# The opening of a fused attention and feed-forward kernel: v of the first head pair on the SP queue, float32 opening matmuls, another order of the first hidden matmuls

## The chip, the cores and the metric

The kernel runs on one core of a Trainium2 chip. The core has TensorE (PE in the profile, with its weight loads listed apart as PEld), VectorE (DVE), ScalarE (ACT), GpSimd (POOL) and SyncE (SP), and 16 DMA engines. The metric is the device time of one execution in microseconds; lower is better. Six runs of the kernel before gave 287.94 to 288.43 us with a median of 288.18 us.

## What is computed

Inputs are float32: q, k, v of shape (8 batches, 8 heads, 576 tokens, 64), g_norm (64), w_in (512, 2048) and w_out (2048, 512). The output has 8 x 576 = 4608 rows of 512.

```python
kv  = einsum('bhsd,bhse->bhde', k, v)          # 64 x 64 per head, no softmax
o   = einsum('bhsd,bhde->bhse', q, kv)
o   = o / sqrt(mean(o*o, -1) + 1e-6) * g_norm  # per token and head
x   = o.transpose(0, 2, 1, 3).reshape(4608, 512)
h   = x @ w_in
out = (h * sigmoid(1.702 * h)) @ w_out
```

## The kernel before

Everything is cast to float16 on the way in and accumulated in float32 in PSUM. Heads go in pairs (`c` = 0 to 3), so that a pair fills 128 partitions. Each batch's first 512 tokens make one tile of the feed-forward part; the last 64 tokens of all eight batches together make a ninth. The 512 model columns are four slices of 128 (`ko` = 0 to 3, which are also the head pairs: slice `ko` of `x` is what the attention of pair `ko` leaves), and the 2048 hidden columns are 16 slices (`fo`). `Hidden.mm(ko, fo)` (L432) is one matmul of 128x128 weights `w_in_sb[:, ko, fo]` with 512 columns of `xT`; four of them over `ko` make one slice of `h`, which `gate` (L443) turns into `gT` on ACT. `project` (L468) multiplies `gT` with `w_out`.

The order of the work on each engine is the order of the program text (`manual_schedule`): every engine runs its own instructions strictly in that order, with semaphores where one needs another's result. The main loop over nine tiles `t` runs `dense(t)` on TensorE and puts the attention steps of batch `t + 1` between its matmuls. Batch 0 has no such cover: it is the opening, written out by hand (L548 to L614), and it is what this change is about.

The opening works like this. For each head pair c of batch 0:

- `a0.q(c)` (L386): 12 transposes of `qraw` on TensorE, copied to `qT` by DVE.
- `a0.kv(c)` (L368): 12 small matmuls of `kraw` and `vbuf`, whose sum DVE spreads into the block-diagonal `kvb` (a multiplication with `ones2`).
- `a0.out(c)` (L253): one matmul of `kvb` with `qT`, squared by ACT into `sq`.
- `a0.sums(c)` (L328), `a0.rs(c)` (L341), `a0.apply(c)` (L347): a matmul of `sq` with `ones2`, then Ln and Exp on ACT, then the product on DVE that writes slice c of `xT`.

Between these stand `busy(n)` calls (L556): n matmuls of 128x512 over the zeroed `kvb[1]`, into a PSUM tile that nobody reads. They keep TensorE running. Then `d0` computes the first six slices of `h` for tile 0 (L598 to L614), and the main loop takes over with slice 6.

Loads. Transfers that cast float32 to float16 are issued on POOL's queue (`early_load` L90, `load_w_in` L153, `load_w_out` L189, `load_half` L110); POOL computes the descriptors of each, about 0.63 us per load in the profile. The program keeps eight semaphores for this queue, in turn, so that a transfer waits until the eighth one ahead of it has landed. For pair 0 the kernel uses float32 transfers on the SP queue for k and q instead (L144 to L148), which are then cast on DVE (`kraw`, L551) and ACT (`qraw`, L550). The order on POOL is: v of pair 0, q of pair 1, the identity matrix (`affine_select`, L162) and three memsets of `ones2` (L171 to L173), k and v of pair 1, then q, k, v of pairs 2 and 3, then w_in in five pieces: slices fo 0-3 with ko 0-1, fo 0-3 with ko 2-3, fo 4-5, fo 6-9, fo 10-15 (L177 to L181). After these come w_out and the data of batch 1.

Of the kernel before, what the change touches and what calls it, by code (L numbers as in the profile page):

```python
# [8 lines left out]
F32 = mybir.dt.float32  # L9
# [3 lines left out]
P = 128  # L13
# [3 lines left out]
def kernel(  # L17
# [10 lines left out]
    nc = tc.nc  # L28
# [6 lines left out]
    KO = DM // P  # L35
    EPS = 1e-6
    SM = 512
# [6 lines left out]
    PE_ = 96  # L44
    NJ = S // PE_
    GROUP = 6
# [5 lines left out]
    const = ctx.enter_context(tc.tile_pool(name="const", bufs=1))  # L52
# [7 lines left out]
    ps_o = ctx.enter_context(tc.tile_pool(name="ps_o", bufs=2, space=bass.MemoryType.PSUM))  # L60
# [13 lines left out]
    vbuf = const.tile([P, NPAIR, 2 * NJ * D], F16)  # L74
# [5 lines left out]
    w_in_sb = const.tile([P, KO, DFF], F16)  # L80
# [9 lines left out]
    def early_load(n, b, c0, c1):  # L90
        nc.gpsimd.dma_start(  # L91
            out=raw[n][0:PE_, c0:c1, :].rearrange("p c (l x) -> p (c l) x", l=2),
            in_=early_src(n, b, c0, c1),
        )
# [45 lines left out]


    first = {}
    early_load("v", 0, 0, 1)
    for n in "kq":  # L144
        first[n] = stage.tile([P, H, J * D], F32, name=f"{n}f", tag=f"{n}f")
        first[n] = first[n].rearrange("p h x -> p (h x)")[0:PE_, 0 : 2 * NJ * D]
        dst, src = first[n].rearrange("p (h x) -> p h x", h=2), early_src(n, 0, 0, 1)
        nc.sync.dma_start(out=dst, in_=src)  # L148
    g_row = const.tile([1, D], F32)
    nc.scalar.dma_start(out=g_row, in_=g_norm.unsqueeze(0))  # L150
    nc.vector.memset(ident, 0.0)
    nc.vector.memset(kvb[1], 0.0)
    def load_w_in(f0, f1, k0=0, k1=KO):  # L153
        nc.gpsimd.dma_start(  # L154
            out=w_in_sb[:, k0:k1, f0 * P : f1 * P],
            in_=moe_w_in[k0 * P : k1 * P, f0 * P : f1 * P].rearrange(
                "(ko ki) f -> ki ko f", ki=P
            ),
        )

    early_load("q", 0, 1, 2)
    nc.gpsimd.affine_select(  # L162
        out=ident,
        in_=ident,
# [6 lines left out]
    nc.gpsimd.memset(ones2, 0.0)  # L171
    nc.gpsimd.memset(ones2[0:D, 0:D], 1.0)
    nc.gpsimd.memset(ones2[D:P, D:P], 1.0)  # L173
    for c in range(1, NPAIR):
        for n in "qkv"[c == 1 :]:
            early_load(n, 0, c, c + 1)
    load_w_in(0, 4, 0, 2)  # L177
    load_w_in(0, 4, 2, KO)
# [267 lines left out]
    def dense(t, units1, units2, group, deep, hid=None):  # L446
# [21 lines left out]
        def project(mo, fo):  # L468
# [10 lines left out]
            if fo == FO - 1:  # L479
# [69 lines left out]

    nc.scalar.copy(qraw[0:PE_, 0, :], first["q"])  # L550
    nc.vector.tensor_copy(kraw[0:PE_, 0, :], first["k"])  # L551


    idle_ps = ps_h.tile([P, SM], F32, name="idle", tag="hT")

    def busy(n):  # L556
        for _ in range(n):
            nc.tensor.matmul(
                idle_ps,
                kvb[1][:, 0, :],  # L560
                kvb[1].rearrange("p c r -> p (c r)"),
                start=True,
                stop=True,
            )

    busy(12)
    a0.q(0)
    busy(2)
    a0.kv(0)
# [10 lines left out]
    a0.out(1)  # L580
    a0.q(2)
    a0.rs(0)
    busy(1)
    a0.kv(2)
    a0.sums(1)
    a0.apply(0)
    busy(1)
    a0.out(2)
    a0.rs(1)
    a0.q(3)  # L590
# [3 lines left out]
    a0.out(3)  # L594
    a0.rs(2)
    a0.apply(2)
    busy(3)
    d0 = Hidden(0)  # L598
    for fo in range(4):
        d0.mm(0, fo, *((ps_h, "hT") if fo < 3 else (ps_a, "att")))  # L600
        if fo == 2:
            a0.ss(3)
            a0.apply(3)
    for ko in (1, 2):
        for fo in range(4):
            d0.mm(ko, fo)
    for ko in range(KO - 1):
        d0.mm(ko, 4, ps_o, "o")
    for fo in range(GROUP - 1):
        d0.mm(KO - 1, fo)  # L610
    for ko in range(KO):
        d0.mm(ko, GROUP - 1, ps_o, "o")
    for fo in range(GROUP):
        d0.gate(fo)  # L614
    load_w_out(0, 4)
# [12 lines left out]
    nc.gpsimd.dma_start(out=g_all, in_=g_norm.unsqueeze(0).to_broadcast([P, D]))  # L628

    osbs = {}  # L630
    HALVED = (2, 3, 4, 5, 6, 7)
    live = {0: a0}

    def start(b):
# [2 lines left out]
    for t in range(NT):  # L637
# [12 lines left out]
        if t == 0:  # L650
# [8 lines left out]
            for c in range(NPAIR):  # L659
# [4 lines left out]
                o = (32, 35, 50, 53)[c]  # L664
# [5 lines left out]
        elif b < B:  # L670
# [5 lines left out]
            f0 = 5 if t == 1 else 2  # L676
# [48 lines left out]
```

## Time and profile before

| | |
|---|---|
| median of six runs | 288.18 us (287.94 to 288.43) |
| the profiled execution | 288.18 us |
| its span, first to last instruction | 286.4 us |
| granted TensorE clock, mean | 1.000 |
| TensorE matmul busy | 278.7 us (97%) |
| ScalarE busy | 156.1 us (54%) |
| VectorE busy | 118.3 us (41%) |
| GpSimd busy | 57.6 us (20%) |
| DMA moved | 38.61 MB, mean 135 GB/s |

All times in the views are microseconds from the start of the span. A timeline row gives the start, the length, the engine, the line of the kernel, the operation, what it writes and reads, how many instructions were merged, and in brackets how long the engine had been idle and what ended the wait. A row of the DMA queues gives packets, megabytes written and the time that the packets took as a share of 16 engines in that stretch; it can be over 100% since packets overlap in an engine. A row of the DMA issues ends with the time from issue to landing. An f16 load of 144 KB reads 288 KB of float32.

Two things help in reading the rows. First, a matmul's listed length (379 ns for 128x512) holds its latency; the spacing of such matmuls in a run is what they cost, and it is 0.216 us where TensorE is at full speed. Second, "busy" in the last 255 us is nearly the whole of TensorE's time, so only the first 30 us leave TensorE waiting.

### The profile page before, as it was taken

How to read it: one execution, taken by the hardware profiler on the slowest of the kernel's cores; microseconds unless marked ns; L12 is line 12 of the kernel's file. 1: busy time of each engine (PE TensorE's matmuls, PEld its weight loads, DVE VectorE, ACT ScalarE, POOL GpSimd, SP SyncE). 2: the span in 40 equal slices, each digit the busy share in tenths (PEclk: the TensorE clock that was granted, in tenths of full speed). 3: DMA queues.
4: the chain of work that ended last, by engine and by line, in shares of the span. 5: the costliest groups of instructions: out<-in, count | busy, mean ns of one | idle time of the engine just before them, and what ended most of it. 6: DMA issues, size and time to landing. Idle time of an engine off the chain costs nothing.

```text
span 286.4 us, 4353 instructions
## 1 busy us (share of the span) xinstructions
PE 278.7 (97%) x1717; PEld 134.8 (47%) x1717; DVE 118.3 (41%) x229; ACT 156.1 (54%) x273; POOL 57.6 (20%) x83
## 2 busy tenths in 40 slices
PE   7799999999999999999999999999999999999995
PEld 2344554455445544554455445544455444444443
DVE  1460466617671567147713853276427500110001
ACT  2588538866565745584467526763666365016400
POOL 8842362111211121113011401131001100000000
PEclk9999999999999999999999999999999999999999
DMA  8999999996589448972798269925401310020022
GB/s 155 169 205 206 205 227 247 235 271 117 124 171 248 80 108 154 229 145 55 209 198 173 38 206 159 227 45 170 95 2 35 112 76 0 36 88 25 0 73 73
DMA packets 54214, 38.61 MB, mean 135 GB/s; under 512 B 31235, under 2 KB 50947, under 8 KB 54195
## 3 DMA queue, kind: packets, MB, share of 16 engines
q0 software_dynamic: 15168, 15.73, 34.0%
q1 hardware_dynamic: 38624, 22.09, 30.3%
q10 hardware_dynamic: 402, 0.52, 0.6%
q8 instruction: 13, 0.21, 0.3%
q14 instruction: 7, 0.05, 0.1%
HBM read 36.73 MB, written 9.44 MB: 161 GB/s over the span
## 4 chain that ended last, share of the span: by engine, by line
PE 92%; DMA 3%; POOL 3%; issue 1%; DVE 0%; POOLq 0%
PE hT L435 43%; PE o L472 42%; DMA w_in_sb<-in_moe_w_in_dram 3%; PE kvp L224 3%; PE outR L288 2%; PE oh L504 1%; POOL vbuf L91 1%; POOL qraw L91 1%; PE ss L336 1%; POOL kraw L91 1%; PE q L413 0%; PE outT L267 0%; PE outT L256 0%; POOL w_in_sb L154 0%; POOL ident L162 0%
## 5 line engine op out<-in xcount | busy, mean ns | idle before, releaser
L472 PE MATMUL o<-w_out_sb,gT 128*128 128x512 f16 x560 | 130.7, 379 | 0.0
L444 ACT ACTIVATE gT<-hT 128x512 f16<-128x512 f32 x144 | 84.5, 599 | 77.1 <-PE hT L435 77.0
L435 PE MATMUL hT<-xT,w_in_sb 128*128 128x512 f16 x512 | 116.3, 379 | 0.3 <-DMA w_in_sb<-in_moe_w_in_dram 0.2
L435 PEld LDWEIGHTS <-w_in_sb 128*128 128x128 f16 x576 | 54.4, 98 | 63.0 <-DMA w_in_sb<-in_moe_w_in_dram 1.4
L472 PEld LDWEIGHTS <-gT 128*128 128x128 f16 x560 | 52.9, 98 | 56.3
L482 DVE COPY osb<-o 128x512 f32<-128x512 f32 x20 | 13.8, 691 | 62.4 <-PE o L472 62.4
L320 POOL TENSOR_TENSOR x<-xr,g_all 128x512 f16<-128x512 f32 x12 | 15.2, 1270 | 70.2 <-DVE xr L313 52.1
L215 DVE COPY kpad<-kraw 64x576 f16<-64x576 f16 x56 | 25.0, 446 | 1.7 <-DMA kraw<-in_k_dram 0.5
L299 DVE TENSOR_REDUCE sum<-sq 128x8 f32<-128x512 f16 x24 | 15.8, 678 | 19.9 <-ACT sq L296 19.9
L237 DVE CAST kvb<-kvp 64x128 f16<-64x128 f32 x28 | 8.1, 288 | 36.8 <-PE kvp L224 36.6
L313 DVE TENSOR_TENSOR xr<-outR,sum 128x512 f32<-128x512 f32 x24 | 15.5, 686 | 11.1 <-ACT sum L310 11.1
L112 POOL DMA_DIRECT2D kraw<-in_k_dram x16 | 9.9, 624 | 49.1 <-DVE kpad L215 42.8
L112 POOL DMA_DIRECT2D vbuf<-in_v_dram x16 | 9.7, 608 | 35.3 <-PE kvp L224 29.6
L320 DVE TENSOR_TENSOR x<-xr,g_all 128x512 f16<-128x512 f32 x12 | 15.2, 1266 | 0.7
L296 ACT ACTIVATE sq<-outR 128x512 f16<-128x512 f32 x24 | 13.6, 590 | 2.0 <-PE outR L288 1.6
L224 PEld LDWEIGHTS <-kpad 128*128 128x128 f16 x252 | 11.1, 98 | 6.5 <-DVE kpad L215 0.2
L435 PE MATMUL hT<-x_rem,w_in_sb 128*128 128x512 f16 x64 | 14.0, 379 | 0.0
L276 ACT ACTIVATE sq<-outT 128x512 f16<-128x512 f32 (+1 forms) x16 | 7.7, 480 | 10.3 <-PE outT L256 8.9
L338 ACT ACTIVATE ln<-ss,eps_t 128x512 f32<-128x512 f32 (+1 forms) x16 | 9.4, 584 | 5.3 <-PE ss L336 5.3
L482 ACT COPY osb<-o 128x512 f32<-128x512 f32 x15 | 8.7, 581 | 6.3 <-PE o L472 6.3
L224 PE MATMUL kvp<-vbuf,kpad 128*128 128x64 f16 x252 | 11.9, 193 | 0.0
L309 ACT ACTIVATE sum<-sum,eps_t 128x16 f32<-128x16 f32 x12 | 3.7, 308 | 15.0 <-DVE sum L299 14.9
(61 smaller groups left out, 140.3 us busy)
## 6 DMA issues: line engine op xcount, KB each, us to landing
out_dram<-osb SPq DMA_DIRECT2D x12, 512.0 KB, 2.8
qf<-in_q_dram SPq DMA_DIRECT2D x5, 1024.0 KB, 8.6
kraw<-in_k_dram POOLq DMA_DIRECT2D x12, 288.0 KB, 6.0
vbuf<-in_v_dram POOLq DMA_DIRECT2D x12, 288.0 KB, 5.6
w_out_sb<-in_moe_w_out_dram POOLq DMA_DIRECT2D x3, 512.0 KB, 14.8
vbuf<-in_v_dram POOLq DMA_DIRECT2D x8, 144.0 KB, 6.6
out_dram<-osb SPq DMA_DIRECT2D x6, 192.0 KB, 4.0
qf<-in_q_dram POOLq DMA_DIRECT2D x1, 1024.0 KB, 11.6
```

What stands on the lines that cost most here:

```text
L112: nc.gpsimd.dma_start(out=raw[n][l * PH : (l + 1) * PH, c0:c1, 0 : NH * D], in_=srcs[n][b].rearrange("(c l) (p j) d -> l p c (j d)", l=2, ...
L215: nc.vector.tensor_copy(out=kpad[r, c, :, l * D : (l + 1) * D], in_=kraw[r, c, 0 : NH * D].rearrange("p (j d) -> p j d", j=NH),)
L224: nc.tensor.matmul(self.kvp[:, c, :], kpad[:, c, j, :], vbuf[:, c, j * D : (j + 1) * D], start=(j == 0), stop=(j == NH - 1),)
L296: nc.scalar.activation(sq, t, AFT.Square)
L299: nc.vector.tensor_reduce(out=self.sum2[:, j % 2, :], in_=sq.rearrange("p (h d) -> p h d", h=H), op=ALU.add, axis=mybir.AxisListType.X,)
L313: nc.vector.tensor_mul(xr[:, i], self.o[j + i].rearrange("p (h d) -> p h d", h=H), s2[:, i, :].unsqueeze(2).to_broadcast([P, H, D]),)
L320: (nc.vector if i else nc.gpsimd).tensor_mul(self.x16[:, j + i, :].rearrange("p (h d) -> p h d", h=H), xr[:, i], g_all.unsqueeze(1).to_bro ...
L338: nc.scalar.activation(ln[:, 0:n], t[:, 0:n], AFT.Ln, bias=eps_t, scale=1.0 / D)
L435: nc.tensor.matmul(self.h[fo], w_in_sb[:, ko, fo * P : (fo + 1) * P], self.x[:, ko], start=(ko == 0), stop=(ko == KO - 1),)
L444: nc.scalar.activation(self.gT[:, fo, :], self.h[fo], AFT.Gelu_apprx_sigmoid)
L472: nc.tensor.matmul(os[mo], gT[:, fo, mo * P : (mo + 1) * P], w_out_sb[:, fo, :], start=(fo == 0), stop=(fo == FO - 1),)
L482: copy(osb[:, mo, :], os[mo])
```

## The change

Pair 0's v goes onto the SP queue as a third float32 transfer behind k and q, and DVE casts it to `vbuf` (behind the cast of k and ahead of the copy of `qT` of pair 0). POOL's queue loses that load, and q of pair 1 is no longer ahead of the identity and the memsets but behind them. The twelve opening float16 matmuls become three float32 ones over a new zeroed tile. Of the later filler matmuls, the two `busy(1)` go, and `busy(3)` becomes `busy(1)`. The first 24 hidden matmuls are the same, in another order: ko 0, 1, 2, 3 of slices 0 to 3, then slices 4 and 5 whole; before, three matmuls of slice 4 stood between ko 2 and ko 3. Tile 7 is stored with one transfer at its end and not with two.

```diff
-    early_load("v", 0, 0, 1)
-    for n in "kq":
+    for n in "kqv":
         first[n] = stage.tile([P, H, J * D], F32, name=f"{n}f", tag=f"{n}f")
...
     nc.vector.memset(ident, 0.0)
+    zeros = const.tile([P, SM], F32)
+    nc.vector.memset(zeros, 0.0)
     nc.vector.memset(kvb[1], 0.0)
...
-    early_load("q", 0, 1, 2)
     nc.gpsimd.affine_select(
...
     nc.gpsimd.memset(ones2[D:P, D:P], 1.0)
...
     for c in range(1, NPAIR):
-        for n in "qkv"[c == 1 :]:
+        for n in "qkv":
             early_load(n, 0, c, c + 1)
...
     nc.vector.tensor_copy(kraw[0:PE_, 0, :], first["k"])
+    nc.vector.tensor_copy(vbuf[0:PE_, 0, :], first["v"])
...
-    busy(12)
+    for _ in range(3):
+        nc.tensor.matmul(idle_ps, zeros[:, 0:P], zeros, start=True, stop=True)
     a0.q(0)
...
     a0.rs(0)
-    busy(1)
     a0.kv(2)
     a0.sums(1)
     a0.apply(0)
-    busy(1)
     a0.out(2)
...
     a0.apply(2)
-    busy(3)
+    busy(1)
     d0 = Hidden(0)
...
-    for ko in (1, 2):
+    for ko in range(1, KO):
         for fo in range(4):
             d0.mm(ko, fo)
-    for ko in range(KO - 1):
-        d0.mm(ko, 4, ps_o, "o")
-    for fo in range(GROUP - 1):
-        d0.mm(KO - 1, fo)
-    for ko in range(KO):
-        d0.mm(ko, GROUP - 1, ps_o, "o")
+    for fo in range(4, GROUP):
+        for ko in range(KO):
+            d0.mm(ko, fo, ps_o, "o")
...
-    HALVED = (2, 3, 4, 5, 6, 7)
+    HALVED = (2, 3, 4, 5, 6)
```

More of the change, by code (lines that the diff above doesn't have):

```diff
@@ L151 @@
     nc.vector.memset(ident, 0.0)
+    zeros = const.tile([P, SM], F32)
+    nc.vector.memset(zeros, 0.0)
     nc.vector.memset(kvb[1], 0.0)
[L153 to L159, printed above, removed]
-    early_load("q", 0, 1, 2)
     nc.gpsimd.affine_select(
@@ L173, with load_w_in @@
     nc.gpsimd.memset(ones2[D:P, D:P], 1.0)
+    def load_w_in(f0, f1, k0=0, k1=KO):
+        nc.gpsimd.dma_start(
+            out=w_in_sb[:, k0:k1, f0 * P : f1 * P],
+            in_=moe_w_in[k0 * P : k1 * P, f0 * P : f1 * P].rearrange(
+                "(ko ki) f -> ki ko f", ki=P
+            ),
+        )
     for c in range(1, NPAIR):
-        for n in "qkv"[c == 1 :]:
+        for n in "qkv":
             early_load(n, 0, c, c + 1)
```

## The prediction

> **What bounds the kernel now.** I read the chain of waits first, for where TensorE begins to run without a break:
>
> ```profile
> 8.76 0.72 POOL w_in_sb L154
> 9.48 0.20 issue
> 9.68 8.24 DMA w_in_sb<-in_moe_w_in_dram
> 17.92 0.05 issue
> 17.97 5.35 PE hT L435 x24
> ...
> 23.44 6.91 PE hT L435 x32
> ```
>
> From 17.97 us on the chain is TensorE alone. What stands before is one transfer, the second piece of w_in (fo 0-3, ko 2-3), issued at 9.68 and landed at 17.92. So the end moves by what that landing moves, or by TensorE work added behind it. 24 matmuls of 0.216 us are 5.18 us; the row has 5.35, so 0.17 us of waiting is left in it. The timeline of the opening shows that and the neighbours:
>
> ```profile
> 1.33 0.82 POOL L91 DMA_DIRECT2D vbuf<-in_v_dram  x1 [0.88 <-POOLq L709]
> 2.15 0.64 POOL L91 DMA_DIRECT2D qraw<-in_q_dram  x1
> 2.87 0.31 POOL L162 TENSOR_SCALAR_AFFINE_SELECT ident<-ident 128x128 f16<-128x128 f16 x1
> ...
> 9.52 0.38 PE L373 MATMUL kv<-vbuf,kraw 96*64 96x64 f16 x12 [0.80 <-DMA vbuf<-in_v_dram]
> ...
> 14.03 0.38 PE L373 MATMUL kv<-vbuf,kraw 96*64 96x64 f16 x12 [0.71 <-DMA vbuf<-in_v_dram]
> ...
> 16.75 0.69 ACT L338 ACTIVATE ln<-ss,eps_t 128x512 f32<-128x512 f32 x1 [0.28 <-PE ss L336]
> ...
> 18.13 0.75 DVE L350 SCALAR_TENSOR_TENSOR xT<-outT,g_col,rs 128x512 f16<-128x512 f32 x1 [0.88 <-ACT rs L344]
> ...
> 24.98 4.87 PEld L435 LDWEIGHTS <-w_in_sb 128*128 128x128 f16 x24 [0.31 <-DMA w_in_sb<-in_moe_w_in_dram]
> ```
>
> The attention of batch 0 waits for its loads as well (0.80 us for v of pair 1, 0.71 us for pair 3). The last row is the second gate: the weights of slice 10 come with the fifth piece of w_in, which landed just before 24.98 us, when TensorE had only some 0.1 us of work left. Whoever makes TensorE earlier between 18 and 25 us is stopped there. The DMA queues tell whether issue or bandwidth sets the landings (stretches 2.75 to 3.00, 4.00 to 4.25, 4.25 to 4.50 and 5 to 6 us, one row per queue):
>
> ```profile
> q1 hardware_dynamic: 70, 0.10, 105.2%
> ...
> q0 software_dynamic: 21, 0.02, 78.8%
> q1 hardware_dynamic: 30, 0.03, 64.5%
> ...
> q0 software_dynamic: 45, 0.03, 90.4%
> q1 hardware_dynamic: 9, 0.01, 15.3%
> ...
> q0 software_dynamic: 256, 0.18, 124.9%
> ```
>
> q1 is SP's float32 queue, q0 POOL's casting queue. The engines are full from 2.5 us on. POOL issues a trio of loads in 3 x 0.63 = 1.9 us, but kv of pairs 1 and 3 start 4.51 us apart, 2.26 us per trio: the backlog grows, and bandwidth, not POOL, sets the landings.
>
> **The change, part by part.** v of pair 0 by SP. The same 288 KB are read, through the same engines, ahead of the same weights, so to first order no landing moves. Second order: plain float32 runs at 393 GB/s in the window 2.75 to 3.00, so 295 KB take 0.75 us; casting loads write 0.167 MB per us from 5 to 9 us, so 147 KB take 0.88 us: gain 0.12 us. While both queues move, source bytes are (0.02 x 2 + 0.03) and (0.03 x 2 + 0.01) MB per 0.25 us, 0.28 MB/us, against 0.33 with the casting queue alone; the third SP load stretches that overlap by up to 1.2 us: loss 1.2 x 0.05 / 0.28 = 0.2 us.
>
> POOL's first load. q of pair 1 now stands behind identity and memsets, 2.87 to 3.72 us, 0.85 us long. They begin at 0.94 (when DVE has zeroed `ident`) at the earliest, at 1.33 (POOL's first work now) at the latest, so q of pair 1 is issued between 1.79 and 2.18 us; now it is at 2.15, behind v. The nine loads then go out at 0.63 us each and the first w_in piece at about 7.9 instead of 8.75, which only lengthens the backlog; the second piece still waits for v of pair 1 to land (the eighth transfer ahead of it, about 9.4 us) as now. The first casting packets showed at 3.75 us, 2.4 us after the first issue; so now at 4.2 to 4.6 us. SP's queue moved its 0.59 MB by 4.4 us; 0.295 MB more at 0.24 to 0.39 MB/us ends at 4.9 to 5.6. The engines stay fed, and the casting queue's slow start (0.75 us to full rate, as now) lies mostly under it. I charge 0.1 us; bounds -0.3 (all covered and the SP rate holds) to +0.8 (nothing covered). Sum of the loads: -0.1 + 0.2 + 0.1 = +0.2 us.
>
> The cast of v on DVE, 0.56 us by the cast of k, queues ahead of pair 0's `qT` copy (0.46 us) and waits for v's landing: the SP queue's end plus 0.8 us (q: last packet 4.4, cast begun 5.21), 5.7 to 6.4 us. So cast until 6.3 to 7.0, copy until 7.4, kv(0) at 6.3 to 7.0 (now 7.01), its product on DVE until 7.8, out(0) at 7.8 (now 7.97). Cost nothing; the cover is the 0.80 us that kv(1) waits. Without it each 0.1 us late would delay pair 0 alone, as pair 3 waits for its own load again.
>
> The opening matmuls. The zeros take 0.54 us on DVE (twice the 0.27 us of the `kvb` memset), so PE starts at 1.5, not 1.27. The only float32 matmuls in the trace are the two of L573, recorded as four: two records each. Six records at the cold spacing of 0.42 us are 2.5 us, ending at 4.0; as long as the twelve now (4.16 us), they end at 5.7; all at the cold spacing twelve passes take 5.1 us, 6.6. q(0) cannot start before the cast of q (ends 6.04 now, perhaps 0.5 us earlier). Late end: 0.5 us, under the same 0.80 us. Taken: nothing.
>
> The Trainium skill, "FP8 and Floating Point Precision", section TensorE Precision Notes, has true float32 as four passes. That would make twelve passes, the work of `busy(12)`; by the two records of this trace it could be half. No time in the sum hangs on it.
>
> Fillers removed. Each is 0.216 us on TensorE ahead of kv(2), of out(2) and of the hidden matmuls; the first two are followed by waits for loads (0.42 us at kv(2), 0.71 at kv(3)), so they gain nothing. `busy(3)` to `busy(1)` frees 0.43 us, but the first piece of w_in lands at 8.75 + 6.6 = 15.35 us, so the hidden matmuls start 0.2 us earlier at most and ss(3) follows; Ln of pair 3 then starts when ACT is free at 16.46 instead of 16.75, and slice 3 of xT is there at 18.60 instead of 18.88.
>
> The matmul order. Both orders have 16 matmuls behind 17.97. Now three of slice 4 wait for the third piece of w_in (the 0.17 us). Afterwards ko 3 comes at 17.97 + 4 x 0.216 = 18.83 and needs that xT slice: wait 0 to 0.1 us. The third piece is long there at 19.7. Gain 0.1 to 0.2 us, which the fifth piece at 24.9 us takes back. Taken: nothing.
>
> The store of tile 7 as one transfer: the trace has its halves issued from 249 us on and TensorE busy to 283 us with the last tile, so 25 us cover it; the last stores go out from 273 us. Nothing.
>
> Sum: +0.2 us on the profiled execution's 288.18 us, which is also the median: 288.4 us. Within 0.2% (0.58 us, about what this kernel's runs can tell) that is no change.
>
> **Rivals.** (1) Slow TensorE clock, slower. In the trace the first seven fillers load weights 0.42 us apart, from 4.2 us on at half that: TensorE starts at half speed and speeds up after some 3 us of steady work, although the granted clock reads 1.000. The change leaves fewer matmuls to keep it: none between 11 and 12.5 us, two fewer at 15, perhaps a 2 us hole from 4.0 to 6.0. If it runs at half speed when the hidden matmuls begin, the filler, eight hidden and one ss matmul cost 10 x 0.21 = 2.1 us more, of which the wait before 17.97 takes 1.1 (0.67 plus the 0.43 freed); with one or two more slow matmuls +1.3 us: 289.5, and up to 290.5 if the pairs slip too. It decides once the slow stretch reaches past 16 us. For it: the fillers are there. Against it: removed is a tenth of the phase's matmul time.
>
> The Trainium skill, "TensorE: Matmul & The Clock Gate", Part 1 speaks against the change here: half speed is the default, released after a busy window of about 3.4 us and back after an idle one, and Part 4 says that transposes do not count as busy in the same way. By that rule the opening has less counted work than its rows show, and the time would be the 289.5 of this rival; the trace shows only that the present amount suffices.
>
> (2) A hole in the DMA stream, slower. If POOL's first load is issued after 2.6 us, the casting queue starts when SP's is empty: 0.6 to 1.0 us lost for every landing, 288.8 to 289.2.
>
> (3) Faster. The chain of waits runs back through POOL's issues without a gap from 1.33 to 9.48 us. If issue sets the landings after all, one load of 0.82 us less brings w_in that much earlier, down to 287.4; against it, the trios above and the 8.24 us in flight.
>
> (4) The loads come out even and the other edits cancel: that is the forecast's own middle, 288.2.
>
> **How the numbers follow.** Forecast 0.57 (288.0 to 288.75), rival 1 0.18, rival 2 0.17, rival 3 0.08. The range runs from 287.7 to 289.5: it leaves out half of rival 1 and most of rival 3, some 0.15. Slower by over 0.2% (above 288.76): rivals 1 and 2 and the forecast's edge, 0.38; faster (below 287.60): most of rival 3, 0.07; the rest 0.55.
>
> **What would show it.** Right: the second piece of w_in lands at 17.9 to 18.2 us and the fifth at 25.0 to 25.2, unbroken PE from there, kv(1) still waiting for vbuf, out(0) no later than 8.8, filler spacing 0.216 us after 5 us. Wrong: hidden matmuls 0.42 us apart after 15 us (rival 1), a stretch between 4 and 6 us with the DMA share well under 1 (rival 2), or w_in landing before 17.5 (rival 3). Most likely to mislead me: the start of POOL's first load, and the clock.

## The result and the profile after

The changed kernel takes 286.92 us (median of 23 runs, 286.61 to 288.81), the kernel before 288.26 us in the same sessions (49 runs). The ratio is 0.9952 with a 95% interval of 0.9941 to 0.9963: faster by 0.48%, or 1.3 us. The forecast was 288.4 us with no change as the likeliest; the time lies below its range of 287.7 to 289.5. The ratios given with each run come from all its timed runs and those of the kernel before beside it, and differ from the quotient of the medians by up to 0.25%.

The profiled execution took 286.91 us with a span of 285.1 us (before: 288.18 and 286.4). TensorE's last matmul ends at 281.67 us instead of 282.98, and 3.4 to 3.5 us follow it in both, so the whole gain, 1.31 us, lies ahead of that point. The chain of waits of the changed kernel (start, length, what) no longer begins with a piece of w_in:

```profile
7.10 5.99 DMA vbuf<-in_v_dram
13.09 0.14 issue
13.22 0.38 PE kv L374 x12
...
16.98 0.76 DVE xT L351
17.79 4.48 PE hT L436 x20
...
22.38 6.91 PE hT L436 x32
```

The load of v of pair 3 is now what TensorE waits for last; after it the attention of pair 3 runs down to slice 3 of `xT`, whose product on DVE ends at 17.74 us, and unbroken TensorE work begins at 17.79. The timeline of the opening shows the same with the neighbours (start, length, engine, line, operation, and in brackets the wait before it):

```profile
1.54 4.41 PE L570 MATMUL idle<-zeros 128*128 128x512 f32 x6 [1.54 <-DVE zeros L152]
...
1.79 0.82 POOL L91 DMA_DIRECT2D qraw<-in_q_dram  x1
...
2.61 0.64 POOL L91 DMA_DIRECT2D kraw<-in_k_dram  x1
...
6.64 0.72 DVE L553 CAST vbuf<-vf 96x768 f16<-96x768 f32 x1 [1.77 <-DMA vf<-in_v_dram]
...
7.41 0.38 PE L374 MATMUL kv<-vbuf,kraw 96*64 96x64 f16 x12 [0.30 <-DVE vbuf L553]
...
8.37 0.38 PE L257 MATMUL outT<-qT,kvb 128*128 128x512 f16 x1
...
13.22 0.38 PE L374 MATMUL kv<-vbuf,kraw 96*64 96x64 f16 x12 [0.69 <-DMA vbuf<-in_v_dram]
...
15.40 2.11 PE L436 MATMUL hT<-xT,w_in_sb 128*128 128x512 f16 x9
...
17.79 4.48 PE L436 MATMUL hT<-xT,w_in_sb 128*128 128x512 f16 x20 [0.27 <-DVE xT L351]
```

`kv` of pair 3 starts at 13.22 us, before at 14.03: 0.81 us of the gain is there. It waits for its load as it did before (0.69 us against 0.71); the load itself came earlier. From there to the first matmul of slice 6 the kernel before needed 7.40 us and the changed one 7.15: another 0.25 us. Another 0.26 us is one gap of TensorE at 167 us in the profile of before (0.10 us of it listed as idle); nine of the 20 profiles taken have such gaps after the first 30 us (0.04 to 0.87 us listed), eleven have none, and I count it to neither.

Why did the loads come earlier? The queue rows of 8 to 12 us (packets, megabytes written, share of 16 engines), first of the kernel before:

```profile
q0 software_dynamic: 937, 0.66, 120.2%
```

and of the changed kernel:

```profile
q0 software_dynamic: 1103, 0.79, 129.4%
```

In both the engines are listed as full, and nothing else reads in that window. Yet the casting queue writes a fifth more. The 144 KB loads of pairs 1 to 3 follow each other by 0.86 us before and by 0.74 us after (median engine of each load, from the trace's landing events). From 15 to 25 us the two are equal again, 2.05 and 2.06 MB. Profiles of other kernels bear it out: with the loads of before, three more wrote 0.61 to 0.70 MB from 8 to 12 us, with the loads of the change two more wrote 0.78 and 0.80. So the rate of the casting queue, which the forecast held fixed, is what changed.

### The profile page after: what moved, and what is told of

Read it like the earlier page. It is cut to its first block, busy times and chain, and to the rows that moved or that the text cites. A ratio compares the mean times of both kernels' runs of the same rounds, so it can differ in the third digit from the quotient of the medians.

```text
span 285.1 us, 4335 instructions
## 1 busy us (share of the span) xinstructions
PE 278.0 (97%) x1707; PEld 134.9 (47%) x1707; DVE 119.6 (42%) x231; ACT 156.2 (55%) x273; POOL 56.8 (20%) x82
## 4 chain that ended last, share of the span: by engine, by line
PE 93%; DMA 2%; POOL 2%; ACT 1%; DVE 0%; issue 0%
PE hT L436 43%; PE o L473 42%; PE kvp L225 3%; DMA vbuf<-in_v_dram 2%; PE outR L289 2%; PE oh L505 1%; PE ss L337 1%; POOL qraw L91 1%; POOL kraw L91 1%; POOL vbuf L91 0%; ACT rs L345 0%; ACT ln L339 0%; PE q L414 0%; PE outT L268 0%; PE outT L257 0%; DVE xT L351 0%
## 5 line engine op out<-in xcount | busy, mean ns | idle before, releaser
L483 DVE COPY osb<-o 128x512 f32<-128x512 f32 x20 | 13.8, 691 | 62.4 <-PE o L473 62.4
```

The costliest lines, as they stand in the source:

```text
L483: copy(osb[:, mo, :], os[mo])
```

## The experiments

Two questions stood at the start: which part of the change brings the time, and why. The kernel before, run beside each on the same chip, had medians of 288.16 to 288.38 us.

**One part alone.** The loads alone, in the kernel before:

```diff
-    early_load("v", 0, 0, 1)
-    for n in "kq":
+    for n in "kqv":
...
-    early_load("q", 0, 1, 2)
     nc.gpsimd.affine_select(
...
-        for n in "qkv"[c == 1 :]:
+        for n in "qkv":
...
+    nc.vector.tensor_copy(vbuf[0:PE_, 0, :], first["v"])
```

> The kernel before with only the loads of the change: v of pair 0 as third SP load and cast on DVE, q of pair 1 behind the identity and the memsets; float16 fillers, matmul order and stores as before. Theory L (the loads make the whole gain, since the casting queue then runs without long packets): w_in piece 2 lands at 15.6 us, piece 5 at 23.6, time 286.7 to 287.0 us. Rival M (the matmul order and the removed fillers make it): 288.1 to 288.4 us, piece 2 at 17.9.

Measured: 287.32 us, ratio 0.9964 (0.9947 to 0.9981). The loads alone bring 1.0 us, most of the gain but not the whole that theory L expected. Its timeline, TensorE:

```profile
13.71 0.38 PE L371 MATMUL kv<-vbuf,kraw 96*64 96x64 f16 x12 [0.49 <-DMA vbuf<-in_v_dram]
...
16.22 6.42 PE L433 MATMUL hT<-xT,w_in_sb 128*128 128x512 f16 x29
```

29 hidden matmuls run in one piece from 16.22 us: the wait for the second piece of w_in, the forecast's bound, has gone (that piece landed at 16.11 us, before at 17.92). `kv` of pair 0 was as late as 8.19 us here, 1.2 us later than before, and it cost nothing, as pair 3 waits for its own load.

Everything but the loads, that is the changed kernel with v of pair 0 first on the casting queue, k and q on SP:

```diff
-    for n in "kqv":
+    early_load("v", 0, 0, 1)
+    for n in "kq":
...
+    early_load("q", 0, 1, 2)
     nc.gpsimd.affine_select(
...
-        for n in "qkv":
+        for n in "qkv"[c == 1 :]:
...
-    nc.vector.tensor_copy(vbuf[0:PE_, 0, :], first["v"])
```

> The changed kernel with the loads of before: v of pair 0 first on the casting queue, q of pair 1 second, k and q on SP; float32 opening matmuls, fewer fillers, new matmul order and store kept. Theory L: 288.1 to 288.5 us, casting loads 0.86 us apart again and piece 2 of w_in at 17.9 us. Rival M: 286.9 us.

Measured: 289.52 us, ratio 1.0033 (1.0013 to 1.0052): slower, and above what either theory had. The rest of the change costs about 1 us without the loads, and the whole gains 1.3 with them, so the parts don't add up. To see which of the rest costs, first the fewer fillers and the new matmul order, with the float16 opening:

```diff
     a0.rs(0)
-    busy(1)
     a0.kv(2)
...
     a0.apply(0)
-    busy(1)
     a0.out(2)
...
-    busy(3)
+    busy(1)
...
-    for ko in (1, 2):
+    for ko in range(1, KO):
         for fo in range(4):
             d0.mm(ko, fo)
...
+    for fo in range(4, GROUP):
+        for ko in range(KO):
+            d0.mm(ko, fo, ps_o, "o")
```

> The kernel before, its loads and its twelve float16 opening matmuls kept, with the fewer fillers and the new matmul order only (store of tile 7 as before). If removing fillers lets the TensorE clock fall when the loads come late: hidden matmuls 0.43 us apart at the start, 289.0 to 290.0 us. If the float32 opening is what cost the clock in the run with all but the loads: full speed (0.216 us) throughout and 287.9 to 288.3 us, since w_in piece 2 still gates.

Measured: 289.21 us, ratio 1.0027 (1.0011 to 1.0044). Its stretches (start and end, length, busy time and instructions of PE, PEld, DVE, ACT and POOL, then the granted TensorE clock, DMA share and GB/s):

```profile
11.00:14.00 3.00, 1.59 (x24) 0.82 (x24) 1.41 (x3) 1.82 (x4) 2.56 (x4) 0.84 1.27 195
14.00:17.00 3.00, 2.82 (x27) 1.29 (x24) 1.41 (x3) 2.24 (x5) 2.06 (x4) 0.50 1.30 202
17.00:20.00 3.00, 3.00 (x8) 1.06 (x7) 1.12 (x2) 2.06 (x4) 1.29 (x3) 0.52 1.27 206
```

The clock column tells it: TensorE was busy for 1.59 of the 3 us from 11 us on, and was granted half its clock from 13.06 to 19.89 us. There the hidden matmuls are 0.43 us apart. The same stretches of the changed kernel:

```profile
11.00:14.00 3.00, 2.17 (x40) 1.17 (x40) 1.91 (x6) 2.27 (x6) 2.52 (x5) 1.00 1.26 202
14.00:17.00 3.00, 3.00 (x14) 1.28 (x15) 1.37 (x3) 2.95 (x6) 1.85 (x3) 1.00 1.35 202
17.00:20.00 3.00, 2.73 (x14) 1.15 (x13) 2.54 (x3) 2.99 (x5) 0.59 (x1) 1.00 1.21 209
```

With the loads earlier the clock stays full. That the work itself then keeps TensorE busy enough is the likely reason, but the listed busy time alone does not sort the profiles: seven have the clock fall in the opening, with TensorE busy for 1.67 to 2.30 us of the 3.41 us ahead of the fall, and one that kept it (ten late casts, below) has a stretch of that length with 1.79. 11 of 12 timed runs of this experiment, and 11 of 12 of the one before it, have a mean granted clock below 0.996; of the changed kernel none. Of the kernel before it is 59 of 145: its fillers held the clock only just. The half-clock stretches of the opening are 3.41 or 6.83 us long in all seven. The Trainium skill, "TensorE: Matmul & The Clock Gate", Part 1, has windows of about 3.4 us after which an idle TensorE goes back to half speed; the lengths agree, but here TensorE wasn't idle: in the 3.41 us ahead of the fall at 13.06 it was busy for 2.00.

The opening matmuls alone, in the kernel before:

```diff
+    zeros = const.tile([P, SM], F32)
+    nc.vector.memset(zeros, 0.0)
     nc.vector.memset(kvb[1], 0.0)
...
-    busy(12)
+    for _ in range(3):
+        nc.tensor.matmul(idle_ps, zeros[:, 0:P], zeros, start=True, stop=True)
```

> The kernel before with only the opening matmuls as three float32 ones. If the float32 opening costs the clock: hidden matmuls 0.43 us apart at the start, 289 us or more. If it is neutral (same length, fillers behind it keep the clock): 288.0 to 288.5 us. With v of pair 0 on the casting queue the packets over 200 ns should be 35 to 50 again, as in all four profiles with it there, against 5 to 23 with it on SP.

Measured: 288.21 us, ratio 1.0010 (0.9987 to 1.0033), with 55 casting packets over 200 ns. Nothing in the time, as forecast. Then the changed kernel with the old order of the first 24 hidden matmuls:

```diff
-    for ko in range(1, KO):
+    for ko in (1, 2):
         for fo in range(4):
             d0.mm(ko, fo)
-    for fo in range(4, GROUP):
-        for ko in range(KO):
-            d0.mm(ko, fo, ps_o, "o")
+    for ko in range(KO - 1):
+        d0.mm(ko, 4, ps_o, "o")
+    for fo in range(GROUP - 1):
+        d0.mm(KO - 1, fo)
+    for ko in range(KO):
+        d0.mm(ko, GROUP - 1, ps_o, "o")
```

> The changed kernel with the matmul order of before (three matmuls of slice 4 between ko 2 and ko 3). In the changed kernel TensorE waits 0.43 us at ko 3 for slice 3 of xT, while w_in piece 3 is there. If that wait is on the path: 286.5 to 286.7 us (part of it goes to w_in piece 5, which lands at 23.6). If the landings gate anyway: 286.9.

Measured: 286.75 us in 6 runs, ratio 0.9945 (0.9926 to 0.9963), which can't be told from the changed kernel's 0.9952. The order is worth nothing that these runs can see. So about 1.0 us of the gain is the loads'. The other 0.3 to 0.4 us is not assigned: the intervals of the loads alone and of the whole overlap, and no run takes the fillers out of the loads-alone kernel by themselves. The profiles speak against the fillers as its source: from `kv` of pair 3 to the first matmul of slice 6 the loads-alone kernel, with all its fillers, needs 7.04 us and the changed one 7.15. They differ in the landing of v of pair 3 (13.57 and 13.09 us), where the last engine is 1.1 us behind the median one with the loads alone and 0.7 in the changed kernel. What is shown of the fillers is that taking them out, along with the new matmul order, costs 0.8 to 1 us with the loads of before and nothing with the earlier ones.

**Where the load's gain comes from.** Two edits touch the loads: v changes queues, and POOL's small work goes ahead of its first load. First the second alone, with v of pair 0 still on POOL, but behind identity and memsets:

```diff
-    early_load("v", 0, 0, 1)
...
-    early_load("q", 0, 1, 2)
     nc.gpsimd.affine_select(
...
     nc.gpsimd.memset(ones2[D:P, D:P], 1.0)
+    early_load("v", 0, 0, 1)
+    early_load("q", 0, 1, 2)
```

> The kernel before with POOL's identity and memsets moved ahead of v of pair 0 and q of pair 1, so that all ten casting loads are issued without a gap, the first at 1.8 us; v of pair 0 stays a casting load. If the gap of 0.87 us in POOL's issues (between q and k of pair 1) makes the long packets: 287.0 to 287.4 us, casting loads 0.75 us apart. If the first casting load being in flight beside SP's two, or ten casting loads rather than nine, makes them: 288.2 to 288.9 us, since the queue starts 0.5 us later and is no faster.

Measured: 287.61 us, ratio 0.9960 (0.9942 to 0.9978); `kv` of pair 3 at 13.77 us. Then the first alone: v of pair 0 on SP, q of pair 1 still ahead of the identity:

```diff
-    early_load("v", 0, 0, 1)
-    for n in "kq":
+    for n in "kqv":
...
+    nc.vector.tensor_copy(vbuf[0:PE_, 0, :], first["v"])
```

> The kernel before with v of pair 0 on the SP queue and cast on DVE, but q of pair 1 still ahead of the identity and the memsets, so the casting queue starts at 1.33 us with one load and then pauses for 0.87 us. If v on SP alone makes the gain: 286.7 to 287.1 us. If the gap in POOL's issues makes the long packets: 288.0 to 288.5 us, with casting loads 0.86 us apart.

Measured: 287.48 us, ratio 0.9968 (0.9954 to 0.9981); `kv` of pair 3 at 13.62 us. By the medians either edit brings 0.7 to 0.9 us and both together 1.0; the three intervals overlap. From 8 to 12 us the casting queue wrote 0.73 MB in the first and 0.79 in the second. So the gain does not need the SP queue, and either edit alone makes most of it. The reverse was tried too: v of pair 0 uncast, but on POOL's queue, in the changed kernel:

```diff
-        nc.sync.dma_start(out=dst, in_=src)
+        (nc.gpsimd if n == "v" else nc.sync).dma_start(out=dst, in_=src)
```

> The changed kernel with pair 0's v still a float32 transfer cast on DVE, but issued first on POOL's queue in place of third on SP's. If it is the cast in the transfer that makes the long packets: as the changed kernel, 286.8 to 287.1 us. If it is that v stands on POOL's queue, which then starts while SP's queue is still busy: v of pair 3 lands at 13.6 to 13.9 us, 287.5 to 288.0 us.

Measured: 289.55 us, ratio 1.0048 (1.0030 to 1.0065). The casting queue wrote 0.78 MB from 8 to 12 us, as in the changed kernel, and the median engine had v of pair 3 at 12.68 us; but from v of pair 2 on the last engine was some 1.0 us behind, and it ended v of pair 3 at 13.69 (13.09 in the changed kernel). With the fillers gone the clock fell (its mean was below 0.996 in 8 of 8 timed runs), and the time is beyond both expectations. So the queue on which the float32 load goes does not set the rate.

The trace has one more sign. A casting packet of 768 bytes takes 79 ns; up to 26 us, 45 casting packets of the kernel before take over 200 ns (up to 1 us), 5 of the changed kernel. So the next theory was that a load of pair 0 on the casting queue, moved beside SP's loads, makes such long packets. Three runs on it, all on the kernel before but for the loads. q of pair 0 cast first, k and v by SP:

```diff
-    early_load("v", 0, 0, 1)
-    for n in "kq":
+    early_load("q", 0, 0, 1)
+    for n in "kv":
...
-    nc.scalar.copy(qraw[0:PE_, 0, :], first["q"])
+    nc.scalar.copy(vbuf[0:PE_, 0, :], first["v"])
```

> The kernel before with q of pair 0, not v, as the first of ten casting loads; k and v of pair 0 on SP, v cast on ACT. If ten casting loads behind only two SP loads make the long packets, whichever load it is: 30 or more casting packets over 200 ns in the first 26 us, 287.8 to 288.4 us. If it is v of pair 0 itself: under 25, and 287.2 to 287.6 us as in the two runs with the old fillers and v on SP.

Measured: 288.16 us, ratio 0.9984 (0.9957 to 1.0010), 50 long packets. k of pair 0 cast first, v and q by SP:

```diff
-    early_load("v", 0, 0, 1)
-    for n in "kq":
+    early_load("k", 0, 0, 1)
+    for n in "vq":
...
-    nc.vector.tensor_copy(kraw[0:PE_, 0, :], first["k"])
+    nc.vector.tensor_copy(vbuf[0:PE_, 0, :], first["v"])
```

> The kernel before with k of pair 0 as the first of ten casting loads; v and q on SP, v cast on DVE. As the run before this one: 30 or more long casting packets and 287.8 to 288.4 us if the count of casting loads decides, under 25 and 287.2 to 287.6 us if v of pair 0 does.

Measured: 288.55 us, ratio 1.0009 (0.9986 to 1.0033), 61 long packets. It makes no difference to the time which of the three is cast (0.74 and 0.70 MB from 8 to 12 us in these two). And the kernel with POOL's work first, held up until SP's loads are nearly through (the edit is shown against that kernel):

```diff
     nc.gpsimd.memset(ones2[D:P, D:P], 1.0)
+    late = const.tile([P, SM], F32)
+    for _ in range(2):
+        nc.gpsimd.memset(late, 0.0)
     early_load("v", 0, 0, 1)
```

> The kernel with POOL's identity and memsets first and all ten casting loads in one row behind them (e3), with two more memsets on POOL ahead of the first load, so that the first casting packets come at about 4.8 us, as in the changed kernel, when SP's two loads have landed. If the long packets come from the casting queue starting while SP's loads are in flight: under 25 of them, casting loads 0.75 us apart. If ten casting loads behind two on SP make them whatever the start: 33 or more, loads 0.83 us apart or more. The time is 0.6 to 1.2 us over e3 either way, or 1.5 to 2.5 over it where the TensorE clock falls back.

Measured: 289.33 us, ratio 1.0034 (1.0010 to 1.0058). The first casting packet moves at 4.50 us, SP's last load has landed at 4.66, so the two hardly overlap. Yet it has 67 long packets, 0.65 MB from 8 to 12 us, and `kv` of pair 3 at 15.20 us. That the start beside SP's loads makes the queue slow was wrong.

The other way round, q of pair 1 on the SP queue as a fourth load, in the changed kernel with the old matmul order:

```diff
+    q1f = stage.tile([P, H, J * D], F32, name="q1f", tag="vf").rearrange("p h x -> p (h x)")[0:PE_, 0 : 2 * NJ * D]
+    nc.sync.dma_start(out=q1f.rearrange("p (h x) -> p h x", h=2), in_=early_src("q", 0, 1, 2))
...
-        for n in "qkv":
+        for n in "qkv"[c == 1 :]:
...
+    nc.scalar.copy(qraw[0:PE_, 1, :], q1f)
```

> The changed kernel with the matmul order of before and q of pair 1 as a fourth float32 load on SP, cast on ACT; eight casting loads are left. If a float32 load on SP in place of a casting load shortens the opening again: v of pair 3 lands at 12.2 to 12.6 us and the time is 286.1 to 286.5 us. If the gain of v was only the end of the long packets: v of pair 3 at 12.7 to 13.0 us and 286.6 to 286.9 us. If the fourth load holds up pair 1 (its cast on ACT stands ahead of the square of pair 0): 287 us or more.

Measured: 287.88 us, ratio 0.9970 (0.9947 to 0.9992): by the medians worse than the changed kernel, though the intervals overlap. Its timeline:

```profile
9.34 0.83 ACT L554 CAST qraw<-q1f 96x768 f16<-96x768 f32 x1 [3.40 <-DMA q1f<-in_q_dram]
...
10.22 0.45 PE L393 MATMUL q<-ident,qraw 96*64 96x96 f16 x12 [1.24 <-ACT qraw L554]
...
14.37 0.38 PE L376 MATMUL kv<-vbuf,kraw 96*64 96x64 f16 x12 [0.65 <-DMA vbuf<-in_v_dram]
```

The fourth load shares the engines with the casting queue until 9.3 us, holds up pair 1, and leaves three engines 1.4 to 1.7 us behind the median one; later the median engine has written v of pair 3 at 12.46 us, the last at 14.23. So a fourth load on SP added nothing here.

**Is it POOL's issue?** After these runs a third explanation fitted the profiles: the landing of v of pair 3 follows its issue (issued at 7.1, 7.8, 8.1 and 8.8 us, landed at 13.1, 13.7, 13.9 and 15.1). It was put against the first-load theory by a pause of POOL in the middle of its loads, in both kernels:

```diff
     for c in range(1, NPAIR):
+        if c == NPAIR - 1:
+            for _ in range(2):
+                nc.gpsimd.memset(late, 0.0)
         for n in "qkv":
```

> The changed kernel with two POOL memsets (1.12 us, the length measured in the run with ten late casts) between the loads of pair 2 and those of pair 3; nothing else is moved. At that point six casting loads are issued and the first lands only at about 7.1 us, so the queue has some four loads left to read and cannot run dry. Theory A, the reads set the landings (few long packets because pair 0 is not on the casting queue): v of pair 3 still lands at 12.7 to 13.3 us, time 286.9 within 0.3. Theory B, POOL's issue sets the landings: the last load of pair 3 is issued about 1.0 us later (8.1 us instead of 7.1) and lands 0.8 to 1.1 us later, at 13.9 to 14.2; time 287.7 to 288.0, or more if TensorE's clock falls back.

> The kernel before with the same pause of POOL (1.12 us) ahead of the loads of pair 3. Theory A: landings as before (v of pair 3 at 13.9 to 14.6), time 288.2 within 0.3. Theory B: v of pair 3 issued at about 9.2 us instead of 8.1, landing at 15.0 to 15.7, time 289.2 to 289.5.

Measured: 288.97 us, ratio 1.0000 (0.9964 to 1.0036), and 290.25 us, ratio 1.0067 (1.0045 to 1.0089). By the times alone, issue would have won. The timeline of the changed kernel with the pause says otherwise:

```profile
13.19 0.38 PE L378 MATMUL kv<-vbuf,kraw 96*64 96x64 f16 x12 [0.65 <-DMA vbuf<-in_v_dram]
...
15.89 1.15 PE L440 MATMUL hT<-xT,w_in_sb 128*128 128x512 f16 x3 [1.31 <-DMA w_in_sb<-in_moe_w_in_dram]
```

v of pair 3 was issued 1.25 us later (8.35 instead of 7.10) and `kv` starts at 13.19 us, as in the changed kernel. In the other one it was issued 1.0 us later and landed at 13.91 us, before at 13.90. So issue does not set the landings one for one. What came later is the first piece of w_in, by 1.5 and 1.7 us; TensorE waits for it, and the clock falls (mean below 0.996 in 7 of 10 and 9 of 9 runs), in the second kernel's profile already at 12.21 us, ahead of that wait.

The opposite, an earlier issue: the three memsets of `ones2` on DVE, in the kernel before and in the changed one.

```diff
-    nc.gpsimd.memset(ones2, 0.0)
-    nc.gpsimd.memset(ones2[0:D, 0:D], 1.0)
-    nc.gpsimd.memset(ones2[D:P, D:P], 1.0)
+    nc.vector.memset(ones2, 0.0)
+    nc.vector.memset(ones2[0:D, 0:D], 1.0)
+    nc.vector.memset(ones2[D:P, D:P], 1.0)
```

> The kernel before with the three memsets of ones2 on DVE instead of POOL, so that all loads from k of pair 1 on are issued about 0.45 us earlier; v of pair 0 stays the first load of the casting queue. Theory A: ten casting loads, pair 0 among them, as before: v of pair 3 lands at 13.9 to 14.6, time 288.2 within 0.3. Theory B: all landings of pairs 1 to 3 0.3 to 0.45 us earlier, time 287.4 to 287.8.

> The changed kernel with the three memsets of ones2 on DVE, so that POOL's first load is issued at about 1.3 us instead of 1.79. Theory A: nothing, 286.9 within 0.3 (a little worse if the casting queue overlaps the SP queue's loads more). Theory B: landings 0.3 to 0.45 us earlier, time 286.5 to 286.7, which would be the fastest kernel of all.

Measured: 287.54 us, ratio 0.9977 (0.9958 to 0.9995), and 287.73 us, ratio 0.9966 (0.9944 to 0.9988). In the kernel before, with v of pair 0 still the first of ten casting loads, POOL's earlier issue brings 0.7 us, with 20 long packets instead of 45. The rows:

```profile
3.09 0.67 POOL L91 DMA_DIRECT2D kraw<-in_k_dram  x1
...
13.49 0.38 PE L373 MATMUL kv<-vbuf,kraw 96*64 96x64 f16 x12 [0.65 <-DMA vbuf<-in_v_dram]
```

k of pair 1 is issued at 3.09 us (3.66 before) and `kv` of pair 3 starts 0.54 us earlier. So the first-load theory was wrong as well. In the changed kernel the same edit does harm by the medians (0.8 us; the intervals overlap). Its casting queue starts at 4.16 us instead of 4.89, v of pair 0 and q of pair 1 are read side by side, and some engines end up to 2.2 us behind: v of pair 0 lands at 7.94 us (6.62 in the changed kernel), v of pair 3 at 13.80 (13.09).

**Lead.** One figure sorts many of the loads of these profiles. Let a load's lead be the time from the start of its issue on POOL to the start of its reading, the latter taken as the moment when the median engine has written the load before it. For the 127 casting loads of pairs 1 to 3 that begin after 6.8 us, in the first 18 profiles:

| lead, us | loads | mean time of one, us |
|---|---|---|
| under 3.3 | 27 | 0.94 |
| 3.3 to 3.6 | 15 | 0.83 |
| 3.6 to 3.9 | 18 | 0.81 |
| 3.9 and more | 67 | 0.75 |

The table holds for the loads read before 11 us. Later ones are quick whatever their lead: over all 20 profiles, the 12 read after 11 us with a lead under 3.9 us took 0.75 us in the mean (0.71 to 0.87), as did the 28 with a longer one; before 11 us it is 0.95 us for the 28 with a lead under 3.3 us and 0.76 for the 45 with 3.9 and more.

In the kernel before, k of pair 1 is issued at 3.66 us and read from 6.14 on, a lead of 2.5 us; the lead grows by what each load takes beyond the 0.63 us of its issue, and reaches 4 us only with pair 3, whose last two loads take 0.75 us. In the changed kernel, k of pair 1 is issued at 2.61 and read from 6.61 on, a lead of 4.0 us, and all that follow have 3.9 to 4.5. The last two runs tested this on new kernels against the first-load theory. More lead with POOL's queue as before: one more load on SP, which nobody reads, in the kernel before.

```diff
+    more = stage.tile([P, H, J * D], F32, name="vf", tag="vf")
+    more = more.rearrange("p h x -> p (h x)")[0:PE_, 0 : 2 * NJ * D]
+    nc.sync.dma_start(out=more.rearrange("p (h x) -> p h x", h=2), in_=early_src("v", 0, 0, 1))
     g_row = const.tile([1, D], F32)
```

> The kernel before with one more float32 load on the SP queue (a second copy of v of pair 0 that nobody reads); POOL's queue is unchanged, with v of pair 0 first. 288 KB more are read, so at an unchanged rate everything from pair 1 on would land 0.7 us later. Theory C (lead): in 127 casting loads of the profiles so far, one that is read 3.9 us or more after its issue began takes 0.75 us, one read within 3.3 us takes 0.94 us; more float32 bytes ahead delay the reads, not the issues, so the lead of pairs 1 to 3 grows from 2.5 to 4.1 us before to 3.4 to 4.2 us and the loads become quicker: 0.72 MB or more written by the casting queue from 8 to 12 us (0.66 before), v of pair 3 landing at 13.3 to 13.9 us in spite of the added bytes, time 287.8 to 288.3. Theory A (a load of pair 0 on the casting queue makes it slow): 0.66 MB in that window, v of pair 3 at 14.3 to 14.9 us, time 288.8 to 289.5.

And less lead with the changed kernel's loads: the two memsets of a spare tile ahead of POOL's first load.

```diff
     nc.gpsimd.memset(ones2[D:P, D:P], 1.0)
+    late = const.tile([P, SM], F32)
+    for _ in range(2):
+        nc.gpsimd.memset(late, 0.0)
```

> The changed kernel with POOL's first load issued 1.1 us later (two memsets of a spare tile ahead of it), at about 2.9 us. SP's three loads keep the engines reading until 6.1 us, so no hole opens. Theory C (lead): the reads start as before and the issues later, so the lead falls from 4.0 to about 3.2 us and the casting loads slow down from 0.745 to 0.83 to 0.94 us each: 0.70 MB or less from 8 to 12 us (0.79 in the changed kernel), v of pair 3 landing at 13.8 to 14.5 us, time 287.7 to 288.5. Theory A (nine loads, none of pair 0, are quick whenever issued): 0.78 MB or more, v of pair 3 at 13.1 to 13.4 us, time 286.9 to 287.3.

Measured: 288.40 us, ratio 1.0013 (0.9989 to 1.0037), and 289.63 us, ratio 1.0047 (1.0030 to 1.0064). The queue rows of 8 to 12 us, of the kernel before with more on SP:

```profile
q0 software_dynamic: 1124, 0.80, 130.9%
```

and of the changed kernel with POOL late:

```profile
q0 software_dynamic: 977, 0.69, 122.0%
```

The rates have changed places. Ten casting loads with v of pair 0 first, but a lead of 3.5 to 4.1 us for those whose reading begins between 7 and 11 us, write as fast as the changed kernel (0.79) with 7 long packets (the last two, whose issue waited for a landing, had a lead of 3.1 and 3.2 us and still took 0.73 and 0.78); nine loads without it, the four of them behind the first at a lead of 2.7 to 3.7 us, write nearly as slowly as the kernel before (0.66), with 36. What the lead theory expected of the rates held in both. For the second the landing was even later than expected (v of pair 3 at 14.77 us, against 13.09 in the changed kernel and 13.8 to 14.5 expected), and the time beyond the expected 287.7 to 288.5; the clock fell as well (below 0.996 in 4 of 4 timed runs). For the first the landing missed, and the time lies just above the expected 287.8 to 288.3. The median engine had v of pair 3 at 13.15 us in spite of 288 KB more, but the copy and the cast load of v of pair 0, read side by side, left some engines 1.6 us behind and the last one wrote it at 14.73.

## Why the prediction was wrong

**What bounds the kernel.** The chain was read rightly and used too simply. "So the end moves by what that landing moves": the second piece of w_in came 2.30 us earlier (15.62 instead of 17.92 us) and the end 1.31. Behind that gate stood another by only 0.34 us, which is what TensorE had waited for the piece: the attention of pair 3, from the landing of its v. The landing of v, 0.81 us earlier, is the one to count from. The 17.92 us itself hung on one engine: 15 of the 16 had written their part by 16.57.

**The loads, +0.2 us: the step that failed.** "The same 288 KB are read, through the same engines, ahead of the same weights, so to first order no landing moves" takes the casting queue's rate as given, 0.167 MB/us, and puts three second-order terms on it. Measured at v of pair 3, the loads moved the landing by -0.81 us: the reading of k of pair 1 begins 0.47 us later than before (6.61 against 6.14), the eight loads from it on then take 5.75 us instead of 6.85 by the median engine, and the last engine is 0.18 us less behind. The rate went from 0.66 to 0.79 MB in 4 us as POOL's issue got further ahead of the reading; that this is the reason is supported, with exceptions (below). The reading of the queue rows behind that step was wrong too. "The engines are full from 2.5 us on" is a sum of packet times, and slow packets fill it as well as quick ones do: 120.2% went with 0.66 MB and 129.4% with 0.79. And "bandwidth, not POOL, sets the landings" held where POOL paused in the middle (v of pair 3 landed where it had) and failed where POOL began earlier: with the memsets on DVE in the kernel before, v of pair 3 landed 0.54 us sooner.

**POOL's first load.** Issued at 1.79 us, at the early end of 1.79 to 2.18. The first casting packet came at 4.89 us, not 4.2 to 4.6, which cost nothing since SP's third load filled the time. That load's last packets began at 6.06 us, not 4.9 to 5.6; at the forecast's own 0.39 MB/us it would have ended at 5.2 at the earliest, so the 4.9 does not come out of its numbers. The Trainium skill, "DMA: Bandwidth & Descriptors", Specifications, gives a load from GpSimd about 1 us to its first byte; here it is 3.1 us from the start of the issue to the first packet (0.82 of them the issue itself), 2.5 us in the kernel before, and 1.5 us with ten late casts, where SP's loads were nearly through.

**The cast of v, at nothing.** Right in cost, late in its times: v landed at 6.62 us (forecast 5.7 to 6.4), `kv` of pair 0 began at 7.41 (6.3 to 7.0), `out` at 8.37 (7.8). It stays under the bound of 8.8 us that the forecast named. The cover that it named, the wait of `kv` of pair 1, was gone (that began at 8.96 us without a wait); the waits of pairs 2 and 3 (0.36 and 0.69 us) covered it instead. The loads-alone kernel, with `kv` of pair 0 at 8.19, shows that even more is hidden.

**The opening matmuls, at nothing.** Right: they end at 5.95 us, within 4.0 to 6.6, and alone they change nothing (288.21 us). Before TensorE speeds up at some 4 us (until then the float16 fillers of the kernel before are 0.43 us apart) their records begin some 0.85 us apart, two per matmul, so one float32 matmul takes as long as four of the float16 ones: the upper bound's twelve passes, not half of them.

**The fillers, "they gain nothing".** Right with the earlier loads, as far as the runs show (7.15 us from `kv` of pair 3 to slice 6, against 7.04 with all fillers kept); with the loads of before, taking them out costs 0.8 to 1 us (289.21 and 289.52 us). This is rival 1, and its mechanism is shown: half clock from 13 to 20 us, matmuls 0.43 us apart, 289.2 to 289.5 us where the forecast had worked out 289.5. It didn't decide here because the loads of pairs 1 to 3 came earlier, an interaction that the forecast didn't price since it moved no landing. The wait that rival 1 set against the slow matmuls, 0.67 us, is the idle time of the weight loads; by the starts of the matmuls TensorE waited 0.34.

**The matmul order, at nothing.** Right as a sum, by a misreading: the "0.17 us of waiting" in the row of 24 is the latency of its last matmul. From 17.97 us on the matmuls begin 0.216 us apart (one 0.226), so none of slice 4 waited for the third piece of w_in. The wait for slice 3 of `xT`, put at 0 to 0.1 us, is 0.43 us, since the weights no longer come later than the attention does; with the old order the time is the same.

**The store of tile 7, at nothing.** Right: 3.4 to 3.5 us from the last matmul to the end in both profiles.

**Rival 2**, the hole in the stream, did not occur (DMA share 1.10 to 1.31 in each half microsecond from 4 to 6 us). **Rival 3** had the sign, and its mark, w_in before 17.5 us, is what the trace shows. Its mechanism, landings set by POOL's issue, does not hold one for one: a pause of 1.1 us in the middle of the issue left pair 3 where it was, while an earlier start moved it.

What stays open: whether lead itself makes the loads quick, and how. The border is not sharp, and after 11 us there is none. One run stands against it: with v as a float32 load on POOL, the eight loads read from 6.8 us on had leads of only 3.0 to 3.9 us, took 0.73 us in the mean and wrote 0.78 MB from 8 to 12 us. The three loads of pair 3 behind the pause in the changed kernel had a lead of only 3.3 to 3.4 us and took 0.74 to 0.76, and at 3.7 us the last two runs show 0.75 and 1.06 us. That lead is the cause of the rate rests on two runs made for it, one profile each, and on the table; something that goes along with it is not ruled out, and what in the chip makes the wait is not seen in any profile.

## What to carry to other kernels

A DMA share of 100% says that the engines hold packets, not that they move bytes: compare the megabytes of the same window with those of a later, undisturbed one, and where they are lower, look how far the issue of each load runs ahead of its reading. Before taking the last gate of the chain as the bound, look how far behind it the next gate stands, since a larger gain stops there. In these runs filler matmuls that hold the clock could be taken out without a loss only where the loads came early, so the two edits have to be priced together.

## What the runs showed of the hardware that was not expected

- A casting load of 144 KB took 0.75 us where its issue had begun at least 3.9 us before it was read, and 0.94 us where that was under 3.3 us (67 and 27 loads); the difference is confined to loads read before 11 us. Its packets of 768 bytes take 79 ns as a rule; 31 of them took 0.2 to 1 us in the kernel before and 4 in the changed one, up to 26 us.
- Loads of two queues read side by side leave some of the 16 engines behind the median one: by 1.4 to 1.7 us with four loads on SP, by 1.6 us with one more load on SP beside ten casting ones. The gap stays for the rest of the opening, and it is the last engine that a wait is for.
- One instruction fetch of 16 KB (a packet of 0.95 us on one engine, at 15.85 us in the profile of before) goes with the last engine's part of the second piece of w_in landing at 17.92 us, 1.4 us after all but two engines had theirs (16.52). A fetch of that size (0.89 to 0.95 us) is in all 20 profiles between 14.5 and 17.3 us; in eight of them the last engine's part of that piece came 1.0 to 1.7 us after the fifteenth's, in the others at most 0.7. It wasn't tried by itself.
- TensorE was granted half its clock in a stretch in which it was listed as busy for half of the time (1.59 of 3 us from 11 us on, half clock from 13.06), not idle; the changed kernel, busy for 2.17 of the same 3 us, kept the full one. Over all profiles listed busy time does not tell which kept it.
